# Moving the second loads of a fused attention and MLP kernel behind the first key transposes, and its block transposes to other slots

## The chip, the cores and the metric

The kernel runs on one core of a Trainium2 chip. A core has engines with an instruction stream each: TensorE (PE in the profile, its weight loads PEld), VectorE (DVE), ScalarE (ACT), GpSimd (POOL) and SyncE (SP, which issues DMAs and waits). Sixteen DMA engines move data between HBM and the core's memory (SBUF). Matmuls write to PSUM, eight banks that PE fills and DVE or ACT empty. The metric is the device time in microseconds (us) of one execution.

## The reference

For batch 8, 8 heads, 576 positions and head size 64 (inputs q, k, v in float32):

```python
scores = scale * np.matmul(q, k.transpose(0, 1, 3, 2))
thresh = np.max(scores, axis=-1, keepdims=True) - tau
scores = np.where(scores >= thresh, scores, -1000000000.0)
attn = softmax(scores)                       # scores less their maximum, exp, over the sum
x = (attn @ v).transpose(0, 2, 1, 3).reshape(4608, 512)
h = x @ w_in                                 # 512 to 2048
g = h * np.clip(h + 3.0, 0.0, 6.0) / 6.0
out = g @ w_out                              # 2048 to 512
```

Every row of scores is cut at its maximum less tau, so the maximum must be known before the exponentials.

## The kernel before

**Tiling.** A *quad* is four heads of one batch (quad = 2 b + g; b the batch, g the half). `load` (L81) brings a quad's q or k as 128 rows by 18 blocks of 64 columns into a tile `nq` or `nk`; each of these two names has two buffers, taken in turn by quad. DVE transposes 32 by 32 blocks of them into `qT` and `kT` (three buffers each): `transpose_k` (L101) in two parts of 10 and 8 blocks, `transpose_q` (L94) in pieces, mostly columns 0 to 8 and 8 to 18. The first piece of q covers 256 query rows, the second the other 320.

**Slots.** The work is a list of 144 slots, 18 per batch (`queue`, L183): a slot is 128 query rows of one pair of heads. In each batch the order is row tiles 0 and 1 of half 0, tiles 0 and 1 of half 1, then the two slots of the *remainder* (t = 4: the last 64 rows of both halves together; these are slots 8 and 9 of the batch, 26 and 27 for the second batch), then tiles 2 and 3 of both halves.

**One slot.** `burst(n)` (L203) makes the scores of slots n and n + 1 on PE into PSUM. Some of its matmuls also wait for a *relay*, an empty instruction on POOL or SP that waits for an earlier matmul of the burst. `sm_max` (L225, DVE) copies the scores to SBUF and takes the row maximum; `sm_bias` (POOL) makes the threshold from it; `sm_mask` and `sm_exp` (ACT) cut and exponentiate; `sm_recip` (DVE) and `sm_norm` (POOL) normalise to bfloat16 `pn`. The block transposes of `pn` are made by PE for slots 0 to 9 (`pe_transpose`, L274, copied out by DVE at L281 and L282), by DMA for all others. `av_main` and `av_rest` multiply with v (DVE copies the product to `xT` or `xR`, L297 and L306). `mm1` is the product with w_in; its gate is made by ACT or DVE (L330, L332) and DVE (L345). `mm2_part` is the product with w_out; `mm2_out` copies the result out (L364) for the store.

**Order.** The order is written out by hand: every engine runs its instructions in program order, and semaphores hold the data dependences. Two tables, `jobs` and `issues`, say in which slot's turn the block transposes (jobs) and the loads (issues) stand. They are filled at L417 to L429 and L442 to L448: with n0 the first slot of the batch before, `when` names the slots of the key load and the query load, then of the four transposes of a quad (keys part 0, part 1, queries 0 to 8, queries 8 to 18). Quads 0 and 1 have jobs in slots 0 and 2.

Three stretches follow each other. The *start* (L143 to L463): the loads of quads 0 and 1 on the ACT and SP queues, an identity matrix, then `warm_up` (L153), idle transposes on PE whose result nobody reads, here 24 of them, then the first transposes, burst 0 and the first maxima. The first four loads of v on POOL stand behind an empty instruction (`seen`, L451) that waits for the first two key transposes. The *first loop* (L476, slots 0 to 13) goes in steps of two slots: burst n + 2 first, then the jobs of slot n, normalising, the maxima of slots n + 2 and n + 3, idle transposes, products. Loads of slots n and n + 1 are issued in it (for slot 0 in three places). The *second loop* (L528, slots 14 to 143) takes one slot a turn: the maximum of slot n + 1, products, `mm1`, the gate, the output copy, on odd slots from 21 on two parts of `mm2` if there are any, exponentials, the jobs of slot n, normalising, on even slots burst n + 2 last, then stores and loads. So a job of slot n stands on DVE before burst n + 2 in program order, and the two run side by side unless the burst reads what the job writes. After the loops PE finishes what is left of `mm1` and `mm2`.

**Lines that the change touches**, besides the tables: the loads at L143 to L148, `warm_up` at L160, the gate at L451 and burst 0's relay engine at L457. The instructions it moves carry the lines of the helpers: L86 (loads), L96 and L110 (block transposes of q and k), L136 (w_in), L155 (idle transposes), L219 (score matmuls).

Of the kernel before, what the change touches and what calls it, by code (L numbers as in the profile page):

```python
# [20 lines left out]
def kernel(  # L21
# [10 lines left out]
    nc = tc.nc  # L32
# [9 lines left out]
    R, T = 32, S // 32  # L42
# [33 lines left out]
    def at(when, n, job):  # L76
        when.setdefault(n, []).append(job)
# [3 lines left out]
    def load(quad, of, t0=0, t1=T, by=nc.sync):  # L81
        b, g = divmod(quad, 2)
        if (quad, of) not in nat:
            nat[quad, of] = nat_pool.tile([P, T * D], F32, tag=("nq", "nk")[of], name=("nq", "nk")[of])
        src = (q, k)[of][b, 4 * g:4 * g + 4].rearrange("h (r t) d -> (h r) (t d)", r=R)
        by.dma_start(out=nat[quad, of][:, t0 * D:t1 * D], in_=src[:, t0 * D:t1 * D])  # L86
# [7 lines left out]
    def transpose_q(quad, t0, t1):  # L94
        rows = nat[quad, 0][:].rearrange("p (t j w) -> p t j w", j=2, w=32)
        nc.vector.transpose(out=qk_of(quad)[0][:].rearrange("p j (t w) -> p t j w", w=32)[:, t0:t1],  # L96
                            in_=rows[:, t0:t1])
# [3 lines left out]
    def transpose_k(quad, part):  # L101
        first, e = ((0, 5), (10, 4))[part]
        rows = nat[quad, 1][:].rearrange("p (t j w) -> p j t w", j=2, w=32)
        outs = qk_of(quad)[1]
        for j in range(2):
            for_u = rows[:, j, first:first + 2 * e].rearrange("p (u e) w -> p u e w", u=2)
            base = outs[:, j, :]
            o = base[:, 64 * part:64 * part + 64].rearrange("p (u w) -> p u w", u=2)
            o = bass.AP(tensor=o.tensor, offset=o.offset, ap=[list(o.ap[0]), [32, 2], [128, e], [1, 32]])
            last = nc.vector.transpose(out=o, in_=for_u)  # L110
        return last
# [22 lines left out]
    def load_w_in(i):  # L134
        f0 = 512 * i
        nc.gpsimd.dma_start(out=w_in_sb[:, :, f0:f0 + 512],  # L136
                            in_=moe_w_in.rearrange("(ki p) f -> p ki f", p=P)[:, :, f0:f0 + 512])
# [5 lines left out]
    load(0, 1, 0, 10, by=nc.scalar)  # L143
    load(0, 0, 0, 4)
    load(0, 1, 10, T)
    load(0, 0, 4, T)
    load(1, 1)
    load(1, 0)  # L148

    identf = singles.tile([P, P], F32)  # L150
    make_identity(nc, identf)
# [1 line left out]
    def warm_up(count):  # L153
        for _ in range(count):
            nc.tensor.transpose(ps[:, OB, P:2 * P], identf[:], identf[:])  # L155

    blank = nc.const_aps.tensor(0.0, [P, P], F32)
    for _ in range(2):
        nc.tensor.matmul(ps[:, OB, P:2 * P], blank, blank, start=True, stop=True)
    warm_up(24)  # L160
    identb = singles.tile([P, P], BF16)
    nc.vector.tensor_copy(out=identb[:], in_=identf[:])
    three = singles.tile([P, 1], F32)
# [32 lines left out]
    def score_col(n, a):  # L196
        return (512 - OWN if n % 2 else 1024 - P) + 1536 * a

    def behind(one, other):
        tc.add_manual_dep(one.ins, other.ins.name, mybir.DependencyInfo(  # L200
            mybir.DependencyClass.Sync, mybir.DependencyReason.DATA), reason="bank")

    def burst(n, by=nc.gpsimd):  # L203
        steps = ((0, 0, P, 0), (1, 0, OWN, 0), (0, 0, P, 1), None,
                 (0, P, OWN, 0), (1, 0, OWN, 1), (0, P, OWN, 1), (1, OWN, P, 0), (1, OWN, P, 1))
        for step in steps:
            if step is None:
                relay = by.nop()
                behind(relay, mm)
                continue  # L210
            i, k0, w, j = step
            sl = queue[n + i]
            for a in range(2):
                c = 32 * (2 * i + a)
                c0 = score_col(n + i, a) + k0
                for quad, rows, q0 in (((2 * sl.b + sl.g, slice(0, P), sl.t * P),) if sl.t < 4 else
                                       [(2 * sl.b + g, slice(64 * g, 64 * g + 64), 512) for g in range(2)]):
                    qT, kT = qkT[quad]
                    mm = nc.tensor.matmul(ps_flat[rows, c0:c0 + w],  # L219
                                          qT[c:c + 32, j, q0:q0 + rows.stop - rows.start],  # L220
                                          kT[c:c + 32, j, k0:k0 + w], start=(j == 0), stop=(j == 1))
                    if (i, k0) == (1, OWN):
                        behind(mm, relay)
# [193 lines left out]
    for quad in range(2, 2 * B):  # L417
        b, g = divmod(quad, 2)
        n0 = (b - 1) * NSLOT
        when = (((1, 5), (8, 9))[g] if b == 1 else ((-1, 3), (7, 9))[g])  # L420
        for n, of in zip(when, (1, 0)):
            at(issues, n0 + n, lambda quad=quad, of=of: load(quad, of, by=nc.sync if quad < 4 else nc.gpsimd))
        when = (((4, 8, 12, 20), (14, 16, 18, 22)) if b == 1 else ((4, 6, 8, 10), (12, 14, 16, 18)))[g]
        for n, job in zip(when, (lambda quad=quad: transpose_k(quad, 0), lambda quad=quad: transpose_k(quad, 1),
                                 lambda quad=quad: transpose_q(quad, 0, 8), lambda quad=quad: transpose_q(quad, 8, T))):
            at(jobs, n0 + n, job)
# [4 lines left out]
    def v_pieces(b, slots):  # L431
        pieces = []

        def piece(i):
            if not pieces:
                pieces.extend(load_v(b))
            pieces[i]()

        for i, n in enumerate(slots):
            at(issues, n, lambda i=i: piece(i))  # L440

    v_pieces(0, (-1, -1, -1, -1, 0, 0, 0, 0))  # L442
    for b in range(1, B):
        v_pieces(b, (13, 14, 15, 16, 17, 18, 19, 20) if b == 1 else [(b - 1) * NSLOT + n for n in range(8, 24, 2)])
    for i, n in enumerate((0, 1, 2, 3)):
        at(issues, n, lambda i=i: load_w_in(i))
    for i, n in enumerate((4, 6, 8, 10)):
        at(issues, n, lambda i=i: load_w_out(i))  # L448

    first = transpose_k(0, 0)  # L450
    seen = nc.gpsimd.nop()  # L451
    behind(seen, first)
    for issue in issues[-1]:
        issue()
    transpose_k(0, 1)
    transpose_q(0, 0, 4)
    burst(0)  # L457
    transpose_q(0, 4, 8)
    warm_up(15)
    for i in range(2):  # L460
# [202 lines left out]
```

## Time and profile before

| | us |
|---|---|
| median of 3 runs | 499.06 (498.92 to 499.25) |
| the profiled execution | 499.35 |
| its span in the trace | 497.6 |
| PE busy | 484.7 |
| DVE busy | 445.9 |
| ACT busy | 441.5 |
| POOL busy | 294.4 |

The profile is one execution. A timeline row gives the start, the busy time, the engine, the source line, the operation, the tiles it writes and reads, its shape and how many instructions are merged; in brackets stands the engine's idle time before it and what ended it. A row of busy time by stage gives the stage, its length, the busy time (and instructions) of PE, PEld, DVE, ACT and POOL, the granted clock of TensorE, the DMA engines' share and their GB/s. Matmul ends are modelled, so rows of one engine can overlap by a little. Idle time of an engine that is not the bottleneck costs nothing.

### The profile page before, as it was taken

What the parts mean: (1) busy time and instruction counts of PE and PEld (TensorE: products, weight loads), DVE (VectorE), ACT (ScalarE), POOL (GpSimd) and SP (SyncE); (2) the same over time, 40 slices, a digit from 0 to 9 for tenths busy, and PEclk for the clock granted to TensorE, in tenths of its full rate; (3) what the DMA queues carried; (4) which work ended last, traced back from release to release, by engine and by line L of the source; (5) the groups of instructions that cost most, each with busy time, mean ns of one, the idle gap of its engine ahead of it and who ended that gap; (6) DMA issues with size and microseconds to landing.
All of it is one profiled execution on the core that took longest, in us unless ns stands there. A gap on an engine that the chain in (4) does not pass through costs nothing.

```text
span 497.6 us, 17398 instructions
## 1 busy us (share of the span) xinstructions
PE 484.7 (97%) x6807; PEld 359.7 (72%) x6807; DVE 445.9 (90%) x1154; ACT 441.5 (89%) x949; POOL 294.4 (59%) x537
## 2 busy tenths in 40 slices
PE   8998999999999999999999999999999999999996
PEld 7766766777677776777777776777777776777474
DVE  6999998999999999999999999999999998887243
ACT  2999999999999999999999999999999999999231
POOL 3877786666666666666666666666666565555000
PEclk9999999999999999999999999999999999999999
DMA  7999899998999889998989898998999779867421
GB/s 213 166 203 200 140 166 187 220 124 157 178 171 198 119 177 183 223 139 171 175 193 179 140 166 173 204 168 147 183 182 206 130 127 133 137 117 138 89 65 42
DMA packets 192626, 79.98 MB, mean 161 GB/s; under 512 B 171168, under 2 KB 183840, under 8 KB 192544
## 3 DMA queue, kind: packets, MB, share of 16 engines
q1 hardware_dynamic: 175312, 55.34, 62.7%
q0 software_dynamic: 16896, 23.07, 24.3%
q8 instruction: 53, 0.87, 0.7%
q10 hardware_dynamic: 336, 0.46, 0.3%
q14 instruction: 29, 0.24, 0.1%
HBM read 36.70 MB, written 9.44 MB: 93 GB/s over the span
## 4 chain that ended last, share of the span: by engine, by line
PE 79%; DVE 5%; DMA 2%; issue 2%; POOL 1%; ACT 0%; SPq 0%; POOLq 0%; DVEq 0%
PE ps L312 47%; PE ps L219 25%; PE ps L289 7%; DVE s L233 3%; DMA pT<-pn 2%; POOL pn L260 1%; DVE g L345 1%; ACT r L330 0%; DVE osb L364 0%; DMA out_dram<-osb 0%; DVE r L332 0%; DVE pR L282 0%; SPq L379 0%; POOL v L119 0%; DVE xT L297 0%
## 5 line engine op out<-in xcount | busy, mean ns | idle before, releaser
L260 POOL TENSOR_SCALAR pn<-s,rinv 128x576 bf16<-128x576 f32 x288 | 211.6, 748 | 16.0 <-DVE rinv L255 1.6
L233 DVE TENSOR_SCALAR_CACHE_REDUCE s<-ps 128x576 f32<-128x576 f32 x288 | 205.0, 750 | 16.6 <-PE ps L219 12.7
L247 ACT ACTIVATE s<-s,bias 128x576 f32<-128x576 f32 x288 | 205.7, 762 | 8.8 <-POOL bias L242 8.7
L252 ACT ACTIVATE s<-s 128x576 f32<-128x576 f32 x288 | 192.3, 671 | 0.0
L219 PE MATMUL ps<-kT,qT 32*128 32x128 f32 (+3 forms) x2560 | 167.7, 414 | 4.3 <-DVE s L233 4.1
L219 PEld LDWEIGHTS ps<-kT,qT 32*128 32x128 f32 (+1 forms) x2560 | 124.5, 174 | 48.5 <-DVE s L233 11.0
L312 PE MATMUL ps<-xT,w_in_sb 128*64 128x256 bf16 (+1 forms) x1936 | 133.0, 274 | 0.5 <-DVE xT L297 0.5
L312 PE MATMUL ps<-w_out_sb,g 128*64 128x512 bf16 (+1 forms) x1024 | 131.2, 379 | 0.0
L312 PEld LDWEIGHTS <-w_in_sb 128*64 128x64 bf16 (+1 forms) x1936 | 105.7, 109 | 10.6 <-issue 3.1
L242 POOL TENSOR_SCALAR bias<-m 128x2 f32<-128x2 f32 (+1 forms) x147 | 27.8, 189 | 136.9 <-DVE rinv L255 123.4
L345 DVE SCALAR_TENSOR_TENSOR g<-r,ps 128x512 bf16<-128x512 f32 x128 | 87.3, 684 | 12.0 <-ACT r L330 8.0
L312 PEld LDWEIGHTS <-g 128*64 128x64 bf16 (+1 forms) x1024 | 61.6, 109 | 47.9 <-issue 0.2
L330 ACT ACTIVATE r<-ps,three 128x512 f32<-128x512 f32 x81 | 55.2, 686 | 19.9 <-PE ps L312 19.0
L252 ACT ACTIVATION_READ_ACCUMULATOR s<-s 128x1 f32 x288 | 54.6, 189 | 0.0
L289 PEld LDWEIGHTS <-v 128*64 128x64 bf16 x960 | 41.4, 111 | 16.0 <-issue 4.1
L289 PE MATMUL ps<-pT,v 128*64 128x256 bf16 x640 | 45.4, 273 | 1.6 <-DVE s L233 1.5
L332 DVE TENSOR_SCALAR r<-ps 128x512 f32<-128x512 f32 x63 | 43.3, 688 | 0.7 <-PE ps L312 0.4
L119 POOL DMA_DIRECT2D v<-in_v_dram x64 | 36.9, 578 | 9.3 <-DVE kT L110 5.4
L364 DVE TENSOR_SCALAR osb<-ps 128x512 f32<-128x512 f32 x32 | 21.9, 683 | 9.0 <-DMA out_dram<-osb 6.3
L110 DVE STREAM_TRANSPOSE kT<-nk 128x320 f32<-128x320 f32 (+1 forms) x64 | 26.3, 451 | 1.4 <-DMA nk<-in_k_dram 1.4
L297 DVE CAST xT<-ps 128x256 bf16<-128x256 f32 x64 | 26.0, 406 | 0.4
L96 DVE STREAM_TRANSPOSE qT<-nq 128x640 f32<-128x640 f32 (+2 forms) x33 | 24.5, 747 | 0.0
(35 smaller groups left out, 173.3 us busy)
## 6 DMA issues: line engine op xcount, KB each, us to landing
out_dram<-osb SPq DMA_DIRECT2D x140, 64.0 KB, 2.4
nk<-in_k_dram POOLq DMA_DIRECT2D x12, 576.0 KB, 4.9
nq<-in_q_dram POOLq DMA_DIRECT2D x12, 576.0 KB, 4.9
v<-in_v_dram POOLq DMA_DIRECT2D x32, 80.0 KB, 4.3
v<-in_v_dram POOLq DMA_DIRECT2D x32, 64.0 KB, 3.2
w_in_sb<-in_moe_w_in_dram POOLq DMA_DIRECT2D x4, 512.0 KB, 6.7
w_out_sb<-in_moe_w_out_dram POOLq DMA_DIRECT2D x4, 512.0 KB, 7.5
pT<-pn SPq DMA_TRANSPOSE x120, 4.2
```

The source lines that it names most:

```text
L119: nc.gpsimd.dma_start(out=vsb[b % 2][32 * g:32 * g + 32].rearrange("p (hp a) c -> p a hp c", a=2)[:, a, :, c0 * D:(c0 + count) * D], in_=v ...
L219: mm = nc.tensor.matmul(ps_flat[rows, c0:c0 + w], qT[c:c + 32, j, q0:q0 + rows.stop - rows.start], kT[c:c + 32, j, k0:k0 + w], start=(j == ...
L233: nc.vector.tensor_scalar(out=sl.s[:, i, :], in0=ps_flat[:, c0:c0 + S], scalar1=1.0, scalar2=None, op0=Alu.mult, op1=Alu.max, accum_out=sl ...
L242: nc.gpsimd.tensor_scalar(out=sl.bias[:, of], in0=sl.m[:, of], scalar1=-scale, scalar2=tau, op0=Alu.mult, op1=Alu.add)
L247: nc.scalar.activation(out=s, in_=s, func=Act.Prelu, bias=sl.bias[:, i:i + 1], scale=scale, alpha=REJECT)
L252: nc.scalar.activation(out=s, in_=s, func=Act.Exp, accum_out=sl.rsum[:, i:i + 1])
L260: nc.gpsimd.tensor_scalar(out=pn[:, i, :], in0=sl.s[:, i, :], scalar1=sl.rinv[:, i:i + 1], scalar2=1.0, op0=Alu.mult, op1=Alu.mult)
L289: nc.tensor.matmul(pb[a * 64:(a + 1) * 64, :], vsb[b % 2][:, 2 * hp + a, u * D:(u + 1) * D], pT[:, block, cols], start=(c == 0), stop=(c = ...
L312: nc.tensor.matmul(out[c:c + w], lhsT[:, c:c + w], rhs, start=start, stop=stop)
L330: nc.scalar.activation(out=r, in_=hps, func=Act.Relu, bias=three[:])
L332: nc.vector.tensor_scalar(out=r, in0=hps, scalar1=3.0, scalar2=0.0, op0=Alu.add, op1=Alu.max)
L345: nc.vector.scalar_tensor_tensor(out=out, in0=r, scalar=6.0, in1=hps, op0=Alu.min, op1=Alu.mult)
```

## The change

Of the six loads at the head, three (queries 4 to 18 of quad 0, keys and queries of quad 1) move behind the first two key transposes, gated on SP as v was on POOL; the queries come in two pieces (4 to 8 and 8 to 18), the first ahead of quad 1's keys. The idle transposes before burst 0 go from 24 to 19. Burst 0's relay moves from POOL to SP. The second quarter of w_in is issued in slot 2's turn instead of slot 1's. For quads 2 and 3 and for all later ones the transposes take other slots, and some key and query loads too. Instructions and their number stay the same but for the split load, one gating instruction and the five idle transposes.

```diff
--- before.py
+++ after.py
@@ -143,9 +143,6 @@
     load(0, 1, 0, 10, by=nc.scalar)
     load(0, 0, 0, 4)
     load(0, 1, 10, T)
-    load(0, 0, 4, T)
-    load(1, 1)
-    load(1, 0)
 
     identf = singles.tile([P, P], F32)
     make_identity(nc, identf)
@@ -157,7 +154,7 @@
     blank = nc.const_aps.tensor(0.0, [P, P], F32)
     for _ in range(2):
         nc.tensor.matmul(ps[:, OB, P:2 * P], blank, blank, start=True, stop=True)
-    warm_up(24)
+    warm_up(19)
     identb = singles.tile([P, P], BF16)
     nc.vector.tensor_copy(out=identb[:], in_=identf[:])
     three = singles.tile([P, 1], F32)
@@ -417,10 +414,10 @@
     for quad in range(2, 2 * B):
         b, g = divmod(quad, 2)
         n0 = (b - 1) * NSLOT
-        when = (((1, 5), (8, 9))[g] if b == 1 else ((-1, 3), (7, 9))[g])
+        when = (((1, 4), (7, 9))[g] if b == 1 else ((-1, 5), (7, 9))[g])
         for n, of in zip(when, (1, 0)):
             at(issues, n0 + n, lambda quad=quad, of=of: load(quad, of, by=nc.sync if quad < 4 else nc.gpsimd))
-        when = (((4, 8, 12, 20), (14, 16, 18, 22)) if b == 1 else ((4, 6, 8, 10), (12, 14, 16, 18)))[g]
+        when = (((4, 8, 10, 22), (12, 14, 18, 24)) if b == 1 else ((8, 10, 12, 20), (14, 16, 18, 22)))[g]
         for n, job in zip(when, (lambda quad=quad: transpose_k(quad, 0), lambda quad=quad: transpose_k(quad, 1),
                                  lambda quad=quad: transpose_q(quad, 0, 8), lambda quad=quad: transpose_q(quad, 8, T))):
             at(jobs, n0 + n, job)
@@ -442,19 +439,23 @@
     v_pieces(0, (-1, -1, -1, -1, 0, 0, 0, 0))
     for b in range(1, B):
         v_pieces(b, (13, 14, 15, 16, 17, 18, 19, 20) if b == 1 else [(b - 1) * NSLOT + n for n in range(8, 24, 2)])
-    for i, n in enumerate((0, 1, 2, 3)):
+    for i, n in enumerate((0, 2, 2, 3)):
         at(issues, n, lambda i=i: load_w_in(i))
     for i, n in enumerate((4, 6, 8, 10)):
         at(issues, n, lambda i=i: load_w_out(i))
 
     first = transpose_k(0, 0)
-    seen = nc.gpsimd.nop()
-    behind(seen, first)
+    for by in (nc.sync, nc.gpsimd):
+        behind(by.nop(), first)
+    load(0, 0, 4, 8)
+    load(1, 1)
+    load(0, 0, 8, T)
+    load(1, 0)
     for issue in issues[-1]:
         issue()
     transpose_k(0, 1)
     transpose_q(0, 0, 4)
-    burst(0)
+    burst(0, by=nc.sync)
     transpose_q(0, 4, 8)
     warm_up(15)
     for i in range(2):
```

## The prediction

> **What bounds the kernel now.** I read the page first (busy shares, the chain), then busy time by stage, then the timeline of the start and of the steps around slot 26. A "step" here runs from one score burst to the next, two slots.
>
> ```profile
> span 497.6 us, 17398 instructions
> PE 484.7 (97%) x6807; PEld 359.7 (72%) x6807; DVE 445.9 (90%) x1154; ACT 441.5 (89%) x949; POOL 294.4 (59%) x537
> ```
>
> Three engines are near full, so the share decides nothing; the stage does. Busy time by stage, columns as length, then PE, PEld, DVE, ACT, POOL:
>
> ```profile
> 49.00:79.00 30.00, 29.03 (x385) 20.95 (x377) 28.77 (x78) 29.45 (x66) 22.45 (x42) 1.00 0.98 162
> 79.00:93.90 14.90, 14.69 (x240) 11.22 (x240) 13.71 (x38) 14.60 (x33) 10.90 (x20) 1.00 0.95 181
> 93.90:105.00 11.10, 9.30 (x137) 7.60 (x137) 11.00 (x30) 10.54 (x23) 6.44 (x13) 1.00 1.15 182
> 148.00:161.00 13.00, 11.97 (x178) 9.13 (x172) 12.75 (x36) 12.42 (x27) 8.23 (x16) 1.00 1.03 213
> 161.00:450.00 289.00, 289.00 (x4370) 214.72 (x4372) 277.23 (x714) 275.25 (x598) 181.02 (x329) 1.00 0.91 163
> ```
>
> From 161 to 450 us TensorE has no idle time: whatever PE has gained or lost by 161 us reaches the end unchanged, and nothing behind 161 us can be gained. Before that PE idles in three places: the start, 93.9 to 105 us (1.80 us, DVE busy 11.00 of 11.10) and 148 to 161 us (1.03 us). The start:
>
> ```profile
> 1.56 5.14 PEld L155 LDWEIGHTS ps<-identf 128*128 128x128 f32 x24
> ...
> 5.08 1.56 DVE L110 STREAM_TRANSPOSE kT<-nk 128x320 f32<-128x320 f32 x4 [1.45 <-DMA nk<-in_k_dram]
> 6.56 0.77 DVE L96 STREAM_TRANSPOSE qT<-nq 128x256 f32<-128x256 f32 x2
> 6.67 2.35 POOL L119 DMA_DIRECT2D v<-in_v_dram  x4 [5.35 <-DVE kT L110]
> 7.02 2.04 PEld L219 LDWEIGHTS ps<-kT,qT 32*128 32x128 f32 x32 [0.32 <-DVE qT L96]
> ...
> 9.18 1.62 PEld L155 LDWEIGHTS ps<-identf 128*128 128x128 f32 x15
> ...
> 9.34 0.76 DVE L233 TENSOR_SCALAR_CACHE_REDUCE s<-ps 128x576 f32<-128x576 f32 x1 [2.01 <-PE ps L219]
> ```
>
> The chain is: first keys land, DVE transposes them (1.56), the first queries (0.39), burst 0 (2.23), row maxima. Behind it DVE and PE alternate with 5.2 to 5.6 us a step up to 50 us. Now the lines around burst 26, DVE then PE:
>
> ```profile
> 78.39 0.75 DVE L233 TENSOR_SCALAR_CACHE_REDUCE s<-ps 128x576 f32<-128x576 f32 x1
> ...
> 79.15 0.40 DVE L297 CAST xT<-ps 128x256 bf16<-128x256 f32 x1
> 79.47 0.68 DVE L364 TENSOR_SCALAR osb<-ps 128x512 f32<-128x512 f32 x1
> 80.06 0.76 DVE L110 STREAM_TRANSPOSE kT<-nk 128x256 f32<-128x256 f32 x2
> 81.60 0.76 DVE L233 TENSOR_SCALAR_CACHE_REDUCE s<-ps 128x576 f32<-128x576 f32 x1 [0.78 <-PE ps L219]
> ```
>
> ```profile
> 78.53 0.43 PE L219 MATMUL ps<-kT,qT 32*64 32x128 f32 x4
> 79.21 2.19 PE L219 MATMUL ps<-kT,qT 32*64 32x128 f32 x60 [0.24 <-DVE s L233]
> 81.32 1.06 PE L312 MATMUL ps<-xT,w_in_sb 128*64 128x256 bf16 x16
> ```
>
> Burst 26 starts as soon as the maximum of slot 25 ends (79.14), beside the copy, the output copy and the key transposes, and DVE waits for its end.
>
> **The change, part by part.**
>
> *First keys earlier.* Three loads (1,600 of 2,304 KB) leave the head of the queue. DVE waits 1.45 us for the first keys, and was free at 3.64 (the small memset at 3.58 plus 0.06): at most 1.44 us can be won. The least is nothing: the slices of the DMA view show 0, 53, 227 and 381 GB/s, so 744 KB by 4.5 us, little over the 704 KB of the three loads that stay, so the later ones may have taken hardly any of it. Nearest rows: the 320 KB took 4.3 us from issue to landing in that crowd, 64 KB pieces of v took 3.3 us without it, so some 1.0 us is what the crowd can cost. I take -0.8, short of that because 704 KB still share the engines.
>
> *Five warm-up transposes fewer.* 5 x 0.214 (5.14 / 24) = 1.07 us less on PE, whose last one now ends near 5.95; with burst 0 at 7.02 - 0.8 = 6.2 they are off the path. But pace matters: these transposes take 0.214 us each, the same ones at 9.18 take 0.108 (1.62 / 15), and burst 0 at 7.02 already runs at the later bursts' 2.2 us. So PE doubled its pace between 6.7 and 7.0 us (the clock column says 1.00 throughout and doesn't show it). A burst that starts 0.8 us earlier may start at the slow pace. If the change of pace stays at 6.8, 0.6 us of the burst run at half pace: +0.3. Ends: 0 (the pace changes before 6.2) and +2.2 (the whole burst at half pace). I take +0.3.
> The Trainium skill ("TensorE: Matmul & The Clock Gate", Part 1: The HAM clock gate) speaks against this edit: the gate opens only after a busy window of about 3.4 us, and the windows run freely. By that rule an estimate is an opening anywhere from 4.2 to 7.6 us in a run that starts at 0.8, a cost of 0 to 0.7 us here in place of my 0.3; worse if idle PE time spoils the window. The trace agrees on the doubling, not on the 3.4 us: it shows 6.
>
> *The moved loads themselves.* They start at the end of the first two key transposes (about 5.98 in old time) plus SP's latency. Relative to the chain: 128 KB (q columns 4 to 8) are needed at 8.95 at the latest (0.38 us before the first maximum); the old 128 KB load took 4.5 us in the crowd, 64 KB took 2.4 to 3.3: landing 8.6 to 9.3 (below nothing it can't go, above +1.8 at 4.5 us). Keys and queries of quad 1 are needed at 12.05 and 13.53; 1,600 KB at the 390 GB/s of the slices is 4.1 us, with v's 288 KB beside it, so near 13, and the next maximum had 0.29 us of slack. Charged 0, 0 to +1.8 kept. On SP four issues of 0.42 us stand ahead of burst 0's relay: they end near 7.9, the relay is needed near 8.6. On POOL nothing is queued ahead any more.
>
> *w_in 1 from slot 1 to 2.* On POOL the normalising of slots 0 and 1 moves up by 0.85 us (issue at 17.63 gone), so ACT's 0.51 us wait for the bias at 21.71 shrinks by 0.3; then three issues of 0.77 stand in a row and the bias of slot 6 comes 0.4 later, 0.2 past ACT's need at 27.05. ACT itself waits 0.13 at 48.58, so this is covered: 0, ends -0.3 and +0.2. Loads of keys and queries in other slots (SP idle, POOL 0.6 us each beside 116 us of waiting for DVE): 0.
>
> *Block transposes up to slot 22.* q of quad 2 in step 10 (0.70) falls into DVE's 0.85 us of idle time at 41.25: free. Keys of quad 3 in steps 12 and 14: the burst covers them but for 0.08 gained at 53.08. Step 16 loses 0.76; its maximum at 58.53 can move up only to the burst's end (58.22): -0.18. Step 20 loses 0.84; maximum at 70.23, burst end near 70.0: -0.08. Step 22's double job stood under burst 24 already: 0. Sum -0.34. Below, nothing; above, all three jobs' full price, -1.7.
>
> *The wait at burst 26.* The last q blocks of quad 3 move from step 22 to step 24. Slots 26 and 27 are the remainder rows, which read exactly those blocks, and burst 26 follows the job in program order; in the built order its second matmul now waits for DVE where it waited for the maximum before. So it can't start at 79.14 but after copy (0.32), output copy (0.59), and the transposes (0.83): 79.14 + 0.08 + 1.74 = 80.96, end 83.2 instead of 81.4: +1.8. PE has nothing else (in order); behind it stand the next products, the maximum of slot 26 and with it ACT's bias. Ends: +2.0 (its first 4 matmuls repeated too) and 0 (if DVE came 1.8 us early). From there PE is full up to 93.9, so it passes on.
>
> *Later.* Steps 28 and 30 get lighter transposes, step 32 a heavier one: -0.06, -0.07 (the burst's end limits it), 0. Step 48: -0.2. From 161 on all steps hold the same eight transposes in 9; the heaviest pair, output copy plus 0.90 keys, runs today without PE idling: 0. Sum -0.33, ends -1.0 and +0.3 if a step overflows.
>
> Sum: -0.8 + 0.3 + 0 - 0.34 + 1.8 - 0.33 = +0.63. The profiled execution took 499.35 us, 1.75 around its span of 497.6, and lies 0.29 above the median of 499.06; so 499.98 by its own time, **499.7** against the median. A change under 0.2% (1.0 us) can hardly be told from none here.
>
> **The rivals.**
> A. *The first keys don't come earlier.* For it: 744 KB moved by 4.5 us. Then PE stands idle from 5.95 to 7.0 and may start burst 0 slow: 0 + 0.6 - 0.34 + 1.8 - 0.33 = +1.7, 500.8 us. Against: the 1.0 us between crowded and lone landings.
> B. *A faster kernel: the wait at burst 26 is absorbed.* Place: 79 to 81 us. It decides if DVE reaches that job 1.8 us earlier relative to PE, which needs the 1.6 us of jobs taken from steps 16 and 20 to come through in full. Then -0.8 + 0.3 - 0.34 - 0.33 = -1.17, 497.9 us. Against: both jobs stood under a burst, and the maximum before burst 26 itself waits for burst 24.
> C. *The moved loads are late.* DVE stands before the first maximum or before quad 1's queries: +0.5 to +1.8 more, about 500.8 us. Against: the slack worked out above.
>
> **How the numbers follow.** Forecast (498.9 to 500.4) 0.55, A 0.25, B 0.12, C 0.08. Under 498.06: two thirds of B, 0.08. Over 500.06: most of A and C (0.28) and a sixth of the forecast's, 0.37. The rest, 0.55, is the same. The range goes from inside B to A with a little on top: 498.3 to 501.0.
>
> **What would show it.** First key transposes near 4.3 instead of 5.08, burst 0 near 6.2, its length 2.2 (fast pace) or up to 2.9. A PE gap of about 1.8 us before burst 26, named as waiting for DVE's q transposes, with DVE's idle time before the maximum of slot 26 near 2.4 instead of 0.78. PE idle at 94 to 105 about 0.1 less. If there is no gap at burst 26, or the start gains over 1.4 us, the forecast is wrong downwards; if DVE waits for q's second piece, or any step behind 161 us shows PE idle, upwards.

## The result, and the profile after

The changed kernel takes 502.03 us (median of 6 executions, 500.69 to 502.64) where the kernel before takes 499.14 (6 executions, 498.92 to 499.33): a ratio of 1.0056, 95% interval 1.0043 to 1.0069. It is 2.9 us slower; 0.6 us were forecast. Its executions also spread over 2.0 us, those of before over 0.4. The profiled execution took 501.70 us, with a span of 499.9.

The page's head and busy time by stage (columns: length, then PE, PEld, DVE, ACT, POOL, the granted clock, DMA share, GB/s):

```profile
span 499.9 us, 17390 instructions
PE 484.7 (97%) x6797; PEld 359.5 (72%) x6802; DVE 445.8 (89%) x1154; ACT 441.6 (88%) x949; POOL 294.1 (59%) x537
```

```profile
79.00:93.90 14.90, 13.55 (x200) 10.17 (x202) 10.62 (x27) 11.21 (x26) 8.20 (x16) 0.89 0.81 172
93.90:105.00 11.10, 9.54 (x144) 7.55 (x141) 10.86 (x30) 10.62 (x23) 6.85 (x15) 1.00 1.01 186
148.00:161.00 13.00, 12.77 (x186) 9.67 (x184) 12.82 (x35) 12.38 (x27) 8.25 (x15) 1.00 1.33 218
161.00:450.00 289.00, 288.40 (x4350) 214.47 (x4346) 278.63 (x720) 275.84 (x598) 181.52 (x329) 1.00 0.95 164
```

One row stands out: from 79 to 93.9 us PE, DVE and ACT all lost time, and the granted clock is 0.89. Microsecond by microsecond:

```profile
78.00:79.00 1.00, 0.35 (x2) 0.11 (x2) 1.00 (x5) 1.00 (x2) 1.00 (x3) 1.00 0.37 80
79.00:80.00 1.00, 0.00 (x0) 0.00 (x0) 1.00 (x2) 1.00 (x4) 0.83 (x3) 1.00 0.00 0
80.00:81.00 1.00, 0.65 (x26) 0.64 (x34) 0.29 (x1) 1.00 (x3) 1.00 (x2) 1.00 0.83 184
81.00:82.00 1.00, 1.00 (x25) 0.88 (x15) 0.00 (x0) 0.81 (x2) 0.33 (x1) 0.59 1.01 308
82.00:83.00 1.00, 1.00 (x27) 0.59 (x15) 0.00 (x0) 0.00 (x0) 0.00 (x0) 0.50 1.12 227
83.00:84.00 1.00, 1.00 (x24) 0.64 (x14) 0.07 (x1) 0.00 (x0) 0.00 (x0) 0.50 1.19 184
84.00:85.00 1.00, 1.00 (x16) 0.89 (x14) 1.00 (x3) 0.00 (x0) 0.00 (x0) 0.70 1.27 258
```

The timeline at that place, PE and then DVE:

```profile
77.93 0.43 PE L216 MATMUL ps<-kT,qT 32*64 32x128 f32 x2
80.35 3.40 PE L216 MATMUL ps<-kT,qT 32*64 32x128 f32 x62 [2.00 <-DVE qT L96]
83.67 1.50 PE L309 MATMUL ps<-xT,w_in_sb 128*64 128x256 bf16 x16
```

```profile
78.54 0.40 DVE L294 CAST xT<-ps 128x256 bf16<-128x256 f32 x1
78.86 0.68 DVE L361 TENSOR_SCALAR osb<-ps 128x512 f32<-128x512 f32 x1
79.46 0.83 DVE L96 STREAM_TRANSPOSE qT<-nq 128x640 f32<-128x640 f32 x1
83.94 0.76 DVE L230 TENSOR_SCALAR_CACHE_REDUCE s<-ps 128x576 f32<-128x576 f32 x1 [3.64 <-PE ps L216]
```

Two losses follow each other. Burst 26 waits 2.00 us for the query transposes that were moved to slot 24; before, it waited 0.24 us, for a maximum. Then PE works again, but from 81.19 to 84.60 us at half its clock: the burst takes 3.40 us where it took 2.19, the products behind it 1.50 where they took 1.06. The step (a step carries the number of the slot in whose turn it begins: step 24 runs from the start of burst 26 to that of burst 28) is 10.32 us long where it was 6.93: +3.39, of which 1.76 us is longer idle time and 1.63 the slower work.

The start, DVE and PE of the changed kernel:

```profile
4.41 1.56 DVE L110 STREAM_TRANSPOSE kT<-nk 128x320 f32<-128x320 f32 x4 [0.77 <-DMA nk<-in_k_dram]
6.34 2.23 PE L216 MATMUL ps<-kT,qT 32*128 32x128 f32 x32 [0.31 <-DVE qT L96]
8.66 0.76 DVE L230 TENSOR_SCALAR_CACHE_REDUCE s<-ps 128x576 f32<-128x576 f32 x1 [0.84 <-PE ps L216]
13.38 0.71 DVE L96 STREAM_TRANSPOSE qT<-nq 128x512 f32<-128x512 f32 x1 [0.46 <-DMA nq<-in_q_dram]
```

The first key transposes start 0.67 us earlier than in the profile before, and burst 0 runs at the full pace. At 13.38 us DVE waits 0.46 us for the queries of quad 1, where it did not wait before; step 0 is 0.17 us longer for it. From burst 0 to burst 26 the two profiles are then equal within 0.1 us.

So three questions went to the chip: whether slot 24 holds all of the loss, whether the idle time is what slows the clock, and where the 0.67 us of the start went.

### The profile page after: what moved, and what is told of

It reads as the page before. It is cut to its first block, busy times and chain, and to the rows that moved or that the text cites. A ratio compares the mean times of both kernels' runs of the same rounds, so it can differ in the third digit from the quotient of the medians.

```text
span 499.9 us, 17390 instructions
## 1 busy us (share of the span) xinstructions
PE 484.7 (97%) x6797; PEld 359.5 (72%) x6802; DVE 445.8 (89%) x1154; ACT 441.6 (88%) x949; POOL 294.1 (59%) x537
## 4 chain that ended last, share of the span: by engine, by line
PE 82%; DVE 7%; issue 1%; ACT 1%; DMA 0%; SPq 0%; DVEq 0%
PE ps L309 48%; PE ps L216 27%; PE ps L286 7%; DVE s L230 4%; DVE g L342 1%; ACT r L327 1%; DVE osb L361 1%; DMA out_dram<-osb 0%; DVE kT L110 0%; DVE r L329 0%; DVE xT L294 0%; DVE pR L279 0%; SPq L376 0%; DVE qT L96 0%; DVE rinv L252 0%
```

## The experiments

All ten were timed beside the kernel before. "Ratio" goes by all executions, so a single late one weighs in it; the medians don't feel it.

| run | what differs | median us (range, executions) | before us | ratio (95% interval) |
|---|---|---|---|---|
| e1_back22 | changed, last query piece in slot 22 | 498.83 (498.26 to 500.80, 11) | 499.20 | 0.9995 (0.9987 to 1.0004) |
| e2_only24 | before, that piece in slot 24 | 502.44 (501.17 to 502.64, 5) | 499.20 | 1.0061 (1.0049 to 1.0073) |
| e3_fill | changed, gap filled with 18 idle transposes | 500.58 (500.19 to 502.95, 7) | 499.20 | 1.0034 (1.0020 to 1.0048) |
| e9_half | changed, gap filled with 9 | 500.52 (500.16 to 505.53, 9) | 499.08 | 1.0039 (1.0017 to 1.0060) |
| e4_start | before, new start alone | 499.33 (499.14 to 499.63, 11) | 499.20 | 1.0004 (0.9995 to 1.0012) |
| e5_tables | before, new tables, piece in slot 22 | 498.55 (498.37 to 499.22, 11) | 499.11 | 0.9991 (0.9983 to 1.0000) |
| e6_q1first | e1, quad 1's queries loaded first | 498.43 (498.17 to 503.94, 12) | 499.11 | 0.9999 (0.9981 to 1.0017) |
| e7_warm24 | e1, 24 idle transposes | 498.96 (498.21 to 499.60, 11) | 499.11 | 0.9999 (0.9990 to 1.0008) |
| e8_light | e6, lighter steps | 498.17 (498.04 to 498.87, 11) | 499.11 | 0.9982 (0.9974 to 0.9991) |
| e10_oldstart | e8 with the start of before | 498.48 (498.14 to 499.93, 11) | 499.08 | 0.9991 (0.9982 to 1.0000) |

### One number back, and one number alone

```diff
 # e1_back22, against the changed kernel
-        when = (((4, 8, 10, 22), (12, 14, 18, 24)) if b == 1 else ((8, 10, 12, 20), (14, 16, 18, 22)))[g]
+        when = (((4, 8, 10, 22), (12, 14, 18, 22)) if b == 1 else ((8, 10, 12, 20), (14, 16, 18, 22)))[g]
 # e2_only24, against the kernel before
-        when = (((4, 8, 12, 20), (14, 16, 18, 22)) if b == 1 else ((4, 6, 8, 10), (12, 14, 16, 18)))[g]
+        when = (((4, 8, 12, 20), (14, 16, 18, 24)) if b == 1 else ((4, 6, 8, 10), (12, 14, 16, 18)))[g]
```

> The changed kernel with one number put back: quad 3's last query piece stands in slot 22 again, as before, and all else as changed. Theory: the job in slot 24 makes TensorE idle 2.0 us before burst 26 where it was 0.24 (+1.76), and that idle time then halves the granted clock for 3.4 us (+1.6); step 24 took 10.32 us against 6.93 (+3.39). So with the job in slot 22 the time falls by about 3.4 us: 502.0 - 3.4 = 498.6 us (498.3 to 498.9), the granted clock stays at 1.00 from 7 us to the end, and step 24 takes 6.9 us again. Rival: the loss sits in the other moved jobs or in the late loads of the start, and slot 24 is only where it shows: 500 us or more, with the idle time before burst 26 still over 1 us.

> The kernel before with one number changed: quad 3's last query piece in slot 24 instead of 22, nothing else. Theory: the same wait and the same drop of the clock come by themselves: 499.1 + 3.4 = 502.5 us when the clock drops, 500.9 in an execution where it does not, so a spread of over 1 us between executions where the kernel before has 0.4. Rival: the wait needs the other moves beside it (DVE later or earlier by the other jobs); then 499.1 to 500 us, and no half clock.

With the piece back in slot 22, burst 26 waits 0.24 us again (PE, e1_back22) and step 24 takes 6.94 us:

```profile
78.55 2.19 PE L216 MATMUL ps<-kT,qT 32*64 32x128 f32 x60 [0.24 <-DVE s L230]
80.67 1.06 PE L309 MATMUL ps<-xT,w_in_sb 128*64 128x256 bf16 x16
```

The time falls by 3.2 us, to 498.83. Moved alone (e2_only24, PE, and the clock in the eighth column of the rows by stage), the piece costs 3.2 us: the same wait, the same half clock, the same step of 10.32 us.

```profile
80.77 3.34 PE L219 MATMUL ps<-kT,qT 32*64 32x128 f32 x62 [2.00 <-DVE qT L96]
84.04 1.55 PE L312 MATMUL ps<-xT,w_in_sb 128*64 128x256 bf16 x16
```

```profile
81.00:82.00 1.00, 1.00 (x34) 0.93 (x28) 0.37 (x2) 1.00 (x2) 0.23 (x1) 0.84 1.12 208
82.00:83.00 1.00, 1.00 (x17) 0.55 (x8) 0.00 (x0) 0.23 (x1) 0.00 (x0) 0.50 0.62 118
```

So the one number holds the whole loss, and needs none of the other moves. One of its five executions took 501.17 us, 1.3 less than the median. Among the six of the changed kernel, too, one took 500.69 us. Both have a mean granted clock of 1.000 on record where the other nine have 0.996 or 0.997. The clock doesn't fall every time.

### The gap filled

```diff
 # e3_fill, against the changed kernel (e9_half: range(9))
+        if n == 24:
+            for _ in range(18):
+                nc.tensor.transpose(ps[:, HB, P:2 * P], identf[:], identf[:])
         if n % 2 == 0 and n + 2 < len(queue):
             burst(n + 2)
```

> The changed kernel with 18 idle transposes (0.108 us each, 1.94 us) put on TensorE ahead of burst 26, where it stood idle for 2.00 us; they write a bank that nobody reads at that time. The wait for DVE stays. Theory: it is the idle time that halves the clock; with TensorE busy the clock stays at 1.00, burst 26 runs in 2.2 us instead of 3.4, the time is 502.0 - 1.5 = 500.5 us (500.2 to 500.9) and the executions lie within 0.6 us of each other. Rival: burst 26 is slow for another reason (it reads blocks that DVE has only just written, or the transfers of 1.0 to 1.3 share beside it take its reads): the burst stays at 3.4 us and the time at 502.

> The changed kernel with 9 idle transposes (0.97 us) ahead of burst 26 instead of 18: half of the 2.0 us gap is filled, some 1.0 to 1.2 us stay. The kernel before idles 0.70 to 1.25 us within single steps (steps 12, 28 and 30) at a granted clock of 1.00. Theory: the clock falls only when TensorE idles for most of some stretch of 3.4 us, and 1.0 us is not enough: 500.6 us as with 18, step 24 about 8.7 us, clock 1.00 throughout. Rival: any whole idle microsecond at this place lets the clock fall: near 502 us in most executions, and step 24 about 10.3 us.

PE of e3_fill, then of e9_half:

```profile
78.51 2.19 PE L574 MATMUL ps<-identf 128*128 128x128 f32 x18
80.62 2.58 PE L216 MATMUL ps<-kT,qT 32*64 32x128 f32 x64
83.13 1.06 PE L309 MATMUL ps<-xT,w_in_sb 128*64 128x256 bf16 x16
```

```profile
78.31 1.20 PE L574 MATMUL ps<-identf 128*128 128x128 f32 x9
79.45 0.43 PE L216 MATMUL ps<-kT,qT 32*64 32x128 f32 x2
80.81 2.19 PE L216 MATMUL ps<-kT,qT 32*64 32x128 f32 x62 [0.94 <-DVE qT L96]
```

The burst still can't go on before DVE has made its blocks, but it runs at the full pace and the clock stays at 1.00. That separates the two prices: the wait alone costs 500.58 - 498.83 = 1.75 us, the clock another 502.03 - 500.58 = 1.45 us in the median. Work that does nothing made the kernel 1.45 us faster. Half the filling does as well: in the profile of e9_half 0.94 us of idle time in one piece left the clock alone, where 2.00 us did not. By the mean granted clock this holds for eight of its nine executions (0.998 or more); the ninth, 505.53 us with 0.995, is taken up below.

The start of the same profile narrows the limit further. Its clock went up at 3.58 us, and then PE waited 1.71 us for burst 0's blocks, at full clock throughout. PE of e9_half, then rows by stage of e9_half and of the changed kernel:

```profile
6.61 2.23 PE L216 MATMUL ps<-kT,qT 32*128 32x128 f32 x32 [1.71 <-DVE qT L96]
```

```profile
3.58:6.99 3.41, 1.70 (x20) 1.46 (x22) 1.94 (x7) 0.00 (x0) 0.72 (x1) 1.00 0.33 116
```

```profile
77.77:81.18 3.41, 1.41 (x34) 0.95 (x38) 2.52 (x8) 3.41 (x9) 3.24 (x6) 1.00 0.49 113
81.19:84.59 3.40, 3.40 (x54) 2.44 (x39) 0.66 (x1) 0.62 (x1) 0.14 (x1) 0.50 1.14 236
```

The stretches are chosen by the clock record of the trace. In the changed kernel the clock went up at 6.09 us and fell at 81.19, 75.09 us later; in e2_only24 the same 75.09 us lie between 6.58 and 81.67; and 75.09 is 22 times 3.413. The 3.41 us that end with the fall hold the whole gap, and PE is busy for 1.41 us of them. The 3.41 us behind the rise in e9_half hold the whole gap of 1.71 us, PE is busy for 1.70, and the clock stays. As far as single profiles tell, the limit lies between these two. What a gap of 2.0 us does that is divided between two such stretches was not profiled.

The Trainium skill ("TensorE: Matmul & The Clock Gate", Part 1) says that the clock is judged over free-running windows of 3413 ns; the half clock here lasts 3.41 us in both profiles that have it, so this agrees. The windows' free phase would fit the executions in which the clock didn't fall, but none of those was profiled. The same page, under "HAM oscillation", gives as a rule to avoid idle gaps over about 3.4 us; here a gap of 2.0 us was enough, and the measurement decides.

### Where the start's gain went

```diff
 # e4_start, against the kernel before
-    load(0, 0, 4, T)
-    load(1, 1)
-    load(1, 0)
...
-    warm_up(24)
+    warm_up(19)
...
-    seen = nc.gpsimd.nop()
-    behind(seen, first)
+    for by in (nc.sync, nc.gpsimd):
+        behind(by.nop(), first)
+    load(0, 0, 4, 8)
+    load(1, 1)
+    load(0, 0, 8, T)
+    load(1, 0)
...
-    burst(0)
+    burst(0, by=nc.sync)
 # e7_warm24, against e1_back22
-    warm_up(19)
+    warm_up(24)
 # e6_q1first, against e1_back22
     load(1, 1)
-    load(0, 0, 8, T)
     load(1, 0)
+    load(0, 0, 8, T)
```

> The kernel before with the start of the changed one alone: three loads behind the first key transposes, 19 idle transposes, burst 0's relay on SP; the tables and w_in as before. Theory: the 0.67 us by which the first keys' transposes come earlier stay, less 0.17 us for the queries of quad 1, which come late in step 0: 499.1 - 0.5 = 498.6 us (498.4 to 498.8). Rival: the 0.67 us are eaten before 50 us, where DVE and TensorE wait for each other in every step: 499.1 us. Second rival: in some executions burst 0 falls into the slow pace of TensorE, since five idle transposes fewer stand ahead of it: spread up to 0.6 us more than the kernel before has.

> The kernel with the job back in slot 22, and 24 idle transposes before burst 0 as in the kernel before, instead of 19. Theory of the fixed order: TensorE runs its idle transposes at 0.214 us until 5.9 to 6.8 us, so the 24th ends near 6.6 to 6.9 us where burst 0 could start at 6.4: a loss of 0.2 to 0.5 us, 499.0 to 499.3 us. Rival: with 19 TensorE stands idle from 5.9 to 6.4 us, and in some executions the clock opens late for that, which is the one time of 500.8 and the spread; then 24 lose little in the median, and the executions lie within 0.6 us of each other.

> The kernel with the job back in slot 22, and in the start the queries of quad 1 loaded ahead of columns 8 to 18 of quad 0's, instead of behind. Theory: the start alone gained nothing (499.33) because the queries of quad 1 land 13.3 to 14.0 us, after DVE wants them: it waits 0.37, 0.46, 0.60 and 0.86 us for them in four profiles, and 0.08 to 0.57 us of that reach the step. 320 KB ahead of them took some 1.3 us. With the order turned, DVE does not wait there, step 0 takes 5.16 us as before, and the time falls by 0.1 to 0.5 us: 498.83 - 0.3 = 498.5 us, with a spread below that of its base (498.26 to 499.28 but for one). Rival: the queries of quad 0 (columns 8 to 18) are late in their place, in step 2: DVE waits for them there, no gain or a loss up to 0.5.

The start alone is worth nothing: 499.33 against 499.20 us, with a spread of 0.49 us, no wider than that of before. DVE of e4_start shows one reason, that of e6_q1first its cure:

```profile
4.63 1.56 DVE L110 STREAM_TRANSPOSE kT<-nk 128x320 f32<-128x320 f32 x4 [1.00 <-DMA nk<-in_k_dram]
13.75 0.71 DVE L96 STREAM_TRANSPOSE qT<-nq 128x512 f32<-128x512 f32 x1 [0.60 <-DMA nq<-in_q_dram]
```

```profile
11.70 1.55 DVE L110 STREAM_TRANSPOSE kT<-nk 128x320 f32<-128x320 f32 x4
13.17 0.67 DVE L96 STREAM_TRANSPOSE qT<-nq 128x512 f32<-128x512 f32 x1
```

The queries of quad 1, last in the new queue, land after 13.3 us, and DVE waits for them by 0.37 to 0.86 us in the five profiles with 19 idle transposes and this order; step 0 loses 0.08 to 0.57 us by it. With that load ahead of columns 8 to 18 of quad 0, the wait is gone, the later piece is in time as well, and the median is 498.43 us, 0.4 less than its base (0.3 when each is taken against its own runs of before). The profiled execution is a late one (503.94 us), but what made it late lies behind 317 us (below).

The other reason is that the 0.67 us came from two single executions. The next profiles of the *old* start had the first keys sooner, with all six loads at the head (DVE, e5_tables, then e10_oldstart):

```profile
4.51 1.56 DVE L110 STREAM_TRANSPOSE kT<-nk 128x320 f32<-128x320 f32 x4 [0.88 <-DMA nk<-in_k_dram]
```

```profile
4.76 1.56 DVE L110 STREAM_TRANSPOSE kT<-nk 128x320 f32<-128x320 f32 x4 [1.13 <-DMA nk<-in_k_dram]
```

Old start: 5.08, 4.77, 4.51, 4.76 us, mean 4.78. New start, eight profiles: 4.41 to 4.72, mean 4.57. The moved loads buy some 0.2 us on average, not 0.67, and the two groups overlap; the profile of before was the latest of its kind.

With 24 idle transposes the loss against e1_back22 was 0.13 us in the median (0.22 when each is taken against its own runs of before), at or below the lower edge of the 0.2 to 0.5 us expected, and hardly to be told from none where the executions spread over 1.4 us. Their length is not fixed. PE of e7_warm24, e5_tables and e10_oldstart, the same 24 transposes in each:

```profile
1.77 5.25 PE L152 MATMUL ps<-identf 128*128 128x128 f32 x24
6.95 2.23 PE L216 MATMUL ps<-kT,qT 32*128 32x128 f32 x32
```

```profile
1.77 4.33 PE L155 MATMUL ps<-identf 128*128 128x128 f32 x24
6.45 1.84 PE L219 MATMUL ps<-kT,qT 32*128 32x128 f32 x22 [0.35 <-DVE qT L96]
```

```profile
1.77 4.00 PE L155 MATMUL ps<-identf 128*128 128x128 f32 x24
6.70 2.23 PE L219 MATMUL ps<-kT,qT 32*128 32x128 f32 x32 [0.93 <-DVE qT L96]
```

The clock went up at 6.80 us in the first, at 4.93 and 4.26 in the others, and over all twelve profiles between 3.58 and 6.81 us. Where it goes up late, 24 transposes hold burst 0 (6.95 us, though its blocks were there at 6.35); where it goes up early, they end before the keys are ready. So by these rows nineteen save at most 0.6 us in some executions, less if burst 0 then begins before the clock is up, and nothing in others. The rival fell: with 24, too, the executions spread over 1.4 us. Burst 0 ran at the full pace in every profile.

### The tables alone, and a faster version

```diff
 # e5_tables, against the kernel before
-        when = (((1, 5), (8, 9))[g] if b == 1 else ((-1, 3), (7, 9))[g])
+        when = (((1, 4), (7, 9))[g] if b == 1 else ((-1, 5), (7, 9))[g])
...
-        when = (((4, 8, 12, 20), (14, 16, 18, 22)) if b == 1 else ((4, 6, 8, 10), (12, 14, 16, 18)))[g]
+        when = (((4, 8, 10, 22), (12, 14, 18, 22)) if b == 1 else ((8, 10, 12, 20), (14, 16, 18, 22)))[g]
 # e8_light, against e6_q1first
-        when = (((4, 8, 10, 22), (12, 14, 18, 22)) if b == 1 else ((8, 10, 12, 20), (14, 16, 18, 22)))[g]
+        when = {1: ((4, 8, 10, 22), (12, 14, 18, 22)), 2: ((6, 2, 8, 20), (12, 16, 18, 22)),
+                3: ((6, 8, 10, 20), (14, 16, 18, 22))}.get(b, ((8, 10, 12, 20), (14, 16, 18, 22)))[g]
 # e10_oldstart, against e8_light: the lines of e4_start the other way round
```

> The kernel before with the changed tables of block transposes and of key and query loads, but quad 3's last query piece in slot 22; start and w_in as before. Theory: the tables are a gain by themselves. In the profile of the run with the job back in slot 22 the way from burst 0 to the end is 490.12 us against 490.58 before, although 0.08 us are lost there to the late queries of quad 1: 0.54 us in all (0.10 before burst 26, 0.27 from there to 167 us, 0.17 behind). 499.2 - 0.5 = 498.7 us (498.5 to 498.9). Rival: that gain belongs to the start (POOL and SP free of other issues) or to w_in; then 499.1 or more.

> The kernel of the turned load order with lighter steps where DVE was the limit: keys of quad 4 in slots 20 and 24 instead of 26 and 28, its first queries in 26 instead of 30, the first keys of quad 5 in 30 instead of 32, and quad 6's first three jobs in 42, 44 and 46 instead of 44, 46 and 48. Theory: TensorE idles 0.70, 0.87 and 0.16 us in steps 28, 30 and 32 and 0.64 us in step 48 because DVE is full there; without these jobs it idles less, down to what ACT allows (10.6 of 11.1 us busy in that stage): 0.5 us at 28 to 32 and 0.4 us at 48, so 0.5 to 1.2 us less than the kernel of the turned order, near 497.7 us. Rival: ACT or the products are the limit in those steps: the same time within 0.2 us, with the idle time of TensorE unchanged and DVE's larger.

> The fastest kernel so far (turned load order, lighter steps; 498.17 us) with the start of the kernel before put back: all six loads at the head, 24 idle transposes, relay on POOL; w_in 1 stays in slot 2. Theory: the new start, even with its loads in the better order, is worth little, since the first keys land between 4.4 and 4.7 us with it and between 4.5 and 5.1 us without it, and what is left in some executions is the 24 idle transposes that hold burst 0 when the clock opens late: 498.3 to 498.6 us, 0.1 to 0.4 slower than with the new start. Rival: the start is worth the full 0.67 us that the first pair of profiles showed: 498.8 us or more. Second rival: it is worth nothing: 498.2 us.

The tables gain 0.56 us in the median by themselves once the one piece is out of slot 24; with all executions the interval, 0.9983 to 1.0000, just reaches no gain. In the profile the way from burst 0 to burst 26 is 0.10 us shorter, that from burst 26 to the end 0.30.

e8_light is the fastest of all, 0.9982 (0.9974 to 0.9991) of the kernel before, but its gain over e6_q1first is 0.26 us where 0.5 to 1.2 were expected. Stages of e6_q1first, then of e8_light (91 to 97 us is about step 28, 154 to 160 step 48):

```profile
91.10:97.30 6.20, 5.50 (x82) 4.21 (x78) 6.17 (x16) 5.91 (x14) 4.00 (x8) 1.00 1.06 198
153.70:160.30 6.60, 5.77 (x88) 4.45 (x84) 6.57 (x20) 6.31 (x15) 3.96 (x8) 1.00 1.16 183
```

```profile
91.10:97.30 6.20, 5.44 (x82) 4.30 (x80) 5.83 (x16) 5.91 (x14) 3.95 (x8) 1.00 1.08 185
153.70:160.30 6.60, 5.83 (x89) 4.71 (x91) 6.23 (x17) 6.31 (x15) 4.10 (x9) 1.00 1.12 161
```

DVE lost 0.34 us of work in each, PE gained almost none, and ACT (fourth number after the length) stayed at 5.91 of 6.20 and 6.31 of 6.60. Steps 28 and 48 are 0.13 and 0.06 us shorter, step 30 not at all. The rival explains more of it than the theory: DVE was full there, but ACT was close behind. With the old start this kernel takes 498.48 us, as expected, so the start in its better order is worth about 0.3 us here (e6_q1first against e5_tables, on the other tables and with w_in moved as well: 0.1).

Four of the kernels (e1_back22, e3_fill, e6_q1first, e9_half) have one or two executions that lie 1.8 to 5.5 us above their median. One was profiled (e6_q1first, 503.94 us): two steps between 317 and 336 us were 5.5 us longer than in e8_light, at a clock of 1.00, and PE, DVE and POOL waited for transfers:

```profile
326.17 0.74 PE L286 MATMUL ps<-pT,v 128*64 128x256 bf16 x10 [1.27 <-DMA pT<-pn]
```

Three block transposes by DMA took 10 to 17 us to land there, against a median of 4.5 in the changed kernel's profile. Why the queues were slow in that execution was not found. It doesn't speak for all of them: the mean granted clock is 0.997 in the 500.80 us of e1_back22 and 0.995 in the 505.53 us of e9_half, below the 0.998 to 1.000 of the other executions of these two, so there the clock may have fallen as well. They were not profiled. The 78 executions of the kernel before that stand beside the ten runs lie between 498.73 and 499.67 us.

## Why the prediction was wrong

**The wait at burst 26** is the step that failed, by its upper end. Mechanism and size of the wait were right: +1.8 was the term, 1.76 us the profile and 1.75 the difference of e3_fill and e1_back22. But the step ended with "PE has nothing else (in order)" and took that idle time for its own length. Its ends, 0 and +2.0, left out what the idle time does to the clock: +1.63 us in the profile, +1.45 in the median. The prediction did weigh the pace of PE, but only at the start, where PE had not yet run; the same trace showed a half pace there, and a gap of 2 us in full work was the next place to ask for it.

**First keys earlier** (-0.8 of at most -1.44) was too hopeful: about -0.2 over four and eight profiles. Rival A ("the first keys don't come earlier") is nearer to it, and its reason, that little more than the three remaining loads had moved by 4.5 us, holds: 0.74 to 0.79 MB in the four profiles of the old start. The price of 1.0 us for the crowd rested on a row that was misread. The 3.3 us for 64 KB of v were not measured without the crowd: two of those four pieces were issued at 7.39 and 8.47 us, while quad 1's queries were under way until 10.55 us. Measured on the load itself, the 320 KB took 3.75 to 4.31 us with the old start and 3.64 to 3.96 with the new. Reading one execution as the kernel's state was the other error: 5.08 us was the latest of four starts of that kind.

**Five warm-up transposes fewer** (+0.3 for a slow burst 0): 0 in all profiles, since the clock was up before burst 0 began in each. The 6.8 us at which the pace changed came back in one profile only (e7_warm24, 6.80 us); in the other ten it was 3.58 to 6.58 us.

**The moved loads** (charged 0, 0 to +1.8 kept): +0.08 to +0.57 us. The critical one was right by name, the queries of quad 1 "near 13", but the slack was not there. Together the three steps of the start were forecast at -0.5 and measured at +0.13 (e4_start).

**w_in**: 0, as forecast. Step 4 is 0.37 us longer and step 6 0.36 shorter in the profile.

**Block transposes up to slot 22** (-0.34): -0.10. Lightening step 16 did not shorten it (5.87 and 5.86 us), nor step 20 (5.84 both), since burst and products were as late as DVE; step 18 lost 0.11. **Later steps** (-0.33): -0.30 in e5_tables, 0.11 of it behind 161 us, where the prediction saw nothing to gain.

By runs, the sum is now -0.56 (tables) + 0.13 (start) + 1.75 (wait) + 1.45 (clock) = +2.8, against a measured +2.9. Without the clock it would be +1.3, some 500.5 us (e3_fill: 500.58): just above the forecast's own 498.9 to 500.4, and inside the range up to 501.0.

## What to carry to other kernels

Before a producer is moved later, look which consumer stands next to it in program order: a piece that may be late for 120 later slots can be one step too late for the two slots that read it first. An idle gap in TensorE can cost more than its length, since its clock can fall behind it; here 2.0 us cost 3.2, and idle work in the gap won the difference back. And what rests on the phase of one execution, such as the landing of a first load or the time at which the clock goes up, wants several profiles before it is worth a term.

## What the runs showed of the hardware

The clock of TensorE fell to one half after 2.00 us without work in the middle of the kernel, 0.84 and 0.90 us after work had begun again, for 3.41 us (81.19 to 84.60 us in the changed kernel, 81.67 to 85.09 in e2_only24). 1.71 us in one piece at the start of e9_half did not bring it down, nor did 0.94 us at burst 26, nor the 1.24 us that are spread over step 12. Both falls came 22 times 3.413 us after the rise at the start. At the start the clock rose between 3.58 and 6.81 us in twelve profiles, for nearly the same instructions from 0.78 us on.
